# Tokens dealt to partitions in consecutive runs, with z, u and the output in longer rows: attention and a gated layer on one core

## The chip, the cores and the metric

One core of a Trainium2 chip. The metric is the device time of one execution in microseconds (us). Ratios are computed from runs of the same rounds: the mean time of one kernel's fast runs over the mean time of the other's, so a ratio is not quite that of the medians quoted beside it.

## The reference, cut to what matters

```python
# u, v: (8, 3008, 256)  z: (8, 3008, 64)  w_in: (256, 2048)  w_out: (2048, 256), all float32
scores = (1.0 / S) * np.matmul(z, z.transpose(0, 2, 1))
attn = np.maximum(scores, 0.0) ** 2
x = (u * np.matmul(attn, v)).reshape(B * S, D)
h = x @ w_in
return ((h * np.cos(h)) @ w_out).astype(np.float32)      # (24064, 256)
```

Attention sums over all tokens of a batch and nothing depends on a token's place, so any order of tokens will do if z, v, u and the output share it.

## The kernel before, where the change touches it

A batch has 3008 tokens: 23 blocks of 128 and one of 64, which is loaded twice so that it fills 128 partitions. Work goes in 48 slots (8 batches of NC = 6 groups of 512 tokens). A slot has a value phase (`phase_a`, attention times v) and a phase of dense matmuls for earlier slots (`phase_b`). All matmul inputs are float16; loads from GpSimd's queue cast from float32.

```python
    def load_rows(t, src, b, g):                 # v and u: token 128*j + p sits on partition p
        full = 4 if g < NC - 1 else 3
        nc.gpsimd.dma_start(
            t[:, 0:full, :],
            src[b, g * CW:g * CW + full * P, :].rearrange("(j p) d -> p j d", p=P),
        )
        if full == 3:
            for r in range(2):
                nc.gpsimd.dma_start(t[r * H:(r + 1) * H, 3, :], src[b, S - H:S, :])

    def load_v(b, g):
        t = vpool.tile([P, 4, D], FP16, name="v16")       # vpool has 7 buffers, a batch needs 6
        ...
    def emit_turns(due, more=0):                 # transposes of attention pieces A, by SyncE's DMA
        ...
                nc.sync.dma_start_transpose(d.rearrange("p (n j) -> p n j", j=P), a)
    ...
    for s in range(3, NSLOT + 1):
        b, J = s // NC, s % NC
        if s < NSLOT - 2:
            load_u(s + 2)
        ...
            phase_a(s)
        ...
            if J == NC - 2:
                load_v(b + 1, 0)
            if J == NC - 1:                      # the next batch's v, as this batch's buffers come free
                for g in range(1, NC):
                    load_v(b + 1, g)
        ...
        phase_b(s)
```

At the start PE (TensorE) runs seven matmuls on zeros to raise its clock, z of the first batch comes as float32 over the queues of SyncE and ScalarE, is cast, turned on PE, and the first scores go to ScalarE for the relu.

## Time and profile before

| | |
|---|---|
| time, median of 3 (later 6) runs | 1193.71 (1194.28) us |
| PE busy | 1183.3 of 1191.4 us |
| packets under 512 B | 404208 of 479862 |
| queue of SyncE (transposes, output) | 54.4% of the time of 16 DMA engines |
| queue of GpSimd (v, u, z, weights) | 27.3% |

The lines themselves stand in the prediction. Engine shares are averages; what matters is whom PE waits for, and where.

### The profile page before, as it was taken

Reading aid. Unit: us, or ns where it says so; the run is one execution under the profiler, and the core shown is the slowest. Engines: PE = TensorE matmul, PEld = TensorE weight load, DVE = VectorE, ACT = ScalarE, POOL = GpSimd, SP = SyncE. Lnnn points to the kernel's source line nnn. Section 1 sums busy time; section 2 is a strip of 40 time slices with the busy share of each in tenths; the row PEclk is TensorE's granted clock in tenths of the full one; section 3 lists DMA queues with packets and bytes.
Section 4 is the critical chain, followed back from the end, with each engine's and each line's share of the span. In section 5 each row is a group of like instructions: output and inputs, shape, how many; then the busy total and the mean of one; then the engine's idle time right before and its main releaser. Section 6 shows DMA issues by size and latency. Waiting matters only on the chain.

```text
span 1191.4 us, 29044 instructions
## 1 busy us (share of the span) xinstructions
PE 1183.3 (99%) x11887; PEld 727.2 (61%) x11887; DVE 1012.3 (85%) x1302; ACT 794.9 (67%) x927; POOL 690.5 (58%) x717
## 2 busy tenths in 40 slices
PE   9999999999999999999999999999999999999998
PEld 4556665665566656666566665656666566665566
DVE  6899888889988898888988889888888888888776
ACT  7966676667666676667676676666766666666454
POOL 3287746657466573755647556476565665545452
PEclk9999999999999999999999999999999999999999
DMA  9999998569995699946999459973898737964301
GB/s 160 172 170 163 138 147 131 102 121 134 143 130 98 123 140 162 131 84 104 157 147 135 85 104 161 169 119 72 122 164 149 122 71 123 166 125 86 65 20 54
DMA packets 479862, 148.00 MB, mean 124 GB/s; under 512 B 404208, under 2 KB 479472, under 8 KB 479728
## 3 DMA queue, kind: packets, MB, share of 16 engines
q1 hardware_dynamic: 380752, 112.93, 54.4%
q0 software_dynamic: 97440, 32.78, 27.3%
q8 instruction: 93, 1.52, 0.5%
q10 hardware_dynamic: 1536, 0.43, 0.2%
q14 instruction: 41, 0.34, 0.1%
HBM read 66.32 MB, written 24.64 MB: 76 GB/s over the span
## 4 chain that ended last, share of the span: by engine, by line
PE 97%; ACT 1%; DVE 1%; issue 0%; POOL 0%; DVEq 0%; ACTq 0%
PE E L404 27%; PE M L482 23%; PE M L258 20%; PE E L258 19%; PE E L194 5%; PE M L525 1%; ACT r L204 1%; PE M L460 1%; DVE g L415 0%; PE E L664 0%; DVE sm L270 0%; PE E L525 0%; POOL s L433 0%; ACT c L412 0%; DVE o L495 0%
## 5 line engine op out<-in xcount | busy, mean ns | idle before, releaser
L412 ACT ACTIVATE c<-E 128x1024 f16<-128x1024 f32 (+1 forms) x384 | 385.7, 1007 | 216.4 <-PE E L404 214.1
L415 DVE SCALAR_TENSOR_TENSOR g<-E,c 128x1024 f16<-128x1024 f32 (+1 forms) x384 | 458.4, 1195 | 60.6 <-ACT c L412 59.5
L204 ACT ACTIVATE r<-E 128x512 f16<-128x512 f32 (+1 forms) x342 | 327.9, 967 | 112.7 <-PE E L194 106.5
L258 PEld LDWEIGHTS <-v 64*128 64x128 f16 x4512 | 246.3, 94 | 229.3 <-issue 19.4
L404 PE MATMUL E<-x,w_in 128*128 128x512 f16 (+1 forms) x1408 | 354.0, 375 | 0.0
L433 POOL TENSOR_TENSOR s<-g 128x512 f16<-128x512 f16 (+1 forms) x184 | 208.3, 1132 | 188.5 <-DVE g L415 138.7
L258 PE MATMUL M<-A,v 64*128 64x512 f16 (+1 forms) x2256 | 283.0, 372 | 0.2 <-DVE o L495 0.2
L258 PE MATMUL E<-A,v 64*128 64x512 f16 (+1 forms) x2256 | 278.1, 371 | 0.0
L434 POOL TENSOR_TENSOR g<-g 128x512 f16<-128x512 f16 (+1 forms) x184 | 219.5, 1193 | 14.4
L404 PEld LDWEIGHTS <-w_in 128*128 128x128 f16 x1536 | 133.1, 98 | 108.9 <-issue 19.5
L482 PEld LDWEIGHTS <-g 128*128 128x128 f16 x2816 | 172.5, 98 | 40.8
L209 DVE TENSOR_TENSOR A<-r 128x1024 f16<-128x1024 f16 x240 | 174.0, 737 | 15.0 <-ACT r L204 14.3
L286 POOL TENSOR_TENSOR x<-sm,uT 128x512 f16<-128x512 f32 (+1 forms) x43 | 48.6, 1132 | 212.9 <-DVE sm L270 212.5
L482 PEld LDWEIGHTS <-s 128*128 128x128 f16 x2112 | 129.4, 98 | 32.1 <-DVE s L440 0.5
L194 PE MATMUL E<-zT 64*128 64x512 f16 (+4 forms) x684 | 127.6, 355 | 2.0 <-DVE sm L270 0.7
L440 DVE TENSOR_TENSOR s<-s,g 128x1024 f16<-128x1024 f16 (+1 forms) x92 | 100.6, 1094 | 2.1 <-POOL s L433 2.1
L482 PE MATMUL M<-w_mix,s 128*128 128x128 f16 x1408 | 94.0, 219 | 0.3 <-POOL s L433 0.3
L482 PE MATMUL M<-w_mix,g 128*128 128x128 f16 x1408 | 93.6, 219 | 0.0
L482 PE MATMUL M<-w_out,g 128*128 128x128 f16 x1408 | 93.6, 219 | 0.0
L212 DVE TENSOR_TENSOR A<-r 128x512 f16<-128x512 f16 (+1 forms) x102 | 79.6, 781 | 8.9 <-ACT r L204 8.1
L194 PEld LDWEIGHTS <-zT 64*128 64x128 f16 x684 | 38.8, 94 | 38.5 <-issue 4.0
L442 DVE TENSOR_TENSOR s<-g,s 128x1024 f16<-128x1024 f16 (+1 forms) x92 | 60.5, 660 | 0.0
(58 smaller groups left out, 646.9 us busy)
## 6 DMA issues: line engine op xcount, KB each, us to landing
out_dram<-o SPq DMA_DIRECT2D x87, 256.0 KB, 2.2
v<-in_v_dram POOLq DMA_DIRECT2D x40, 256.0 KB, 8.8
u<-in_u_dram POOLq DMA_DIRECT2D x40, 256.0 KB, 4.8
A<-A SPq DMA_TRANSPOSE x252, 5.1
z<-in_z_dram POOLq DMA_DIRECT2D x14, 192.0 KB, 10.6
z<-in_z_dram POOLq DMA_DIRECT2D x14, 176.0 KB, 5.9
v<-in_v_dram POOLq DMA_DIRECT2D x8, 192.0 KB, 11.9
u<-in_u_dram POOLq DMA_DIRECT2D x8, 192.0 KB, 4.1
```

What stands on the lines that cost most here:

```text
L194: nc.tensor.matmul(e[:, t, 0:Wt], zT[rows, k * P:(k + 1) * P], zT[rows, J * CW:J * CW + Wt], start=True, stop=True,)
L204: nc.scalar.activation(r[:, :, 0:W], e[:, :, 0:W], AF.Relu)
L209: nc.vector.tensor_tensor(a4, r4, r4, ALU.mult)
L212: nc.vector.tensor_tensor(a4, r[:, :, 0:W], r[:, :, 0:W], ALU.mult)
L258: nc.tensor.matmul(bank[:, 0:width(J)], vs[b, k // 4][t * H:(t + 1) * H, k % 4, dh * P:(dh + 1) * P], value_rhs(b, J, k, t), start=start, ...
L404: nc.tensor.matmul(e[:, f, 0:W], w_in16[:, k, ft * P:(ft + 1) * P], x[:, k, 0:W], start=(k == 0), stop=(k == 1),)
L412: nc.scalar.activation(c[:, :, 0:W], e[:, :, 0:W], AF.Sin, bias=half_pi, scale=inv_s2)
L415: return lambda: nc.vector.scalar_tensor_tensor(gs[m][:, 2 * i:2 * i + 2, 0:W], e[:, :, 0:W], 1.0, c[:, :, 0:W], ALU.mult, ALU.mult)
L433: nc.gpsimd.tensor_tensor(s1[:, f, 0:n], g[:, f, low], g[:, lower, low], ALU.add)
L434: nc.gpsimd.tensor_tensor(g[:, f, low], g[:, f, up], g[:, f, low], ALU.subtract)
L440: nc.vector.tensor_tensor(s2[:, f, 0:n], s1[:, f, 0:n], g[:, f, up], ALU.subtract)
L482: nc.tensor.matmul(acc[:, k * P:(k + 1) * P], left[:, ft, k * P:(k + 1) * P], right[:, ft, :], start=(ft == 0 and k == 0), stop=(ft == F - ...
```

## The change

The intent is fewer and longer packets. Each half batch (12 or 11 full blocks) is dealt so that partition p owns 12 or 11 consecutive tokens. Four tokens of a partition then lie side by side in HBM, and a transfer can move them as one row where they lie side by side on chip too. v's tile is padded so that its rows don't.

```diff
+    def half_rows(rows, half):
+        lo, hi = halves[half]
+        n = min(hi, NB - 1) - lo
+        return rows[lo * P:(lo + n) * P, :].rearrange("(p j) d -> p j d", p=P)
+
+    def group_rows(rows, g):
+        first = 4 * (g % 3)
+        return half_rows(rows, g // 3)[:, first:first + (4 if g < NC - 1 else 3), :]
 ...
         nc.gpsimd.dma_start(
             t[:, 0:full, :],
-            src[b, g * CW:g * CW + full * P, :].rearrange("(j p) d -> p j d", p=P),
+            group_rows(src[b], g),
         )
 ... (load_z: later z in the same order)
-        t = vpool.tile([P, 4, D], FP16, name="v16")
+        t = vpool.tile([P, 4, D + 16], FP16, name="v16")[:, :, 0:D]
 ... (store_half, last_y: the output)
-            nc.sync.dma_start(
-                out[t0:t0 + n * P, :].rearrange("(k p) d -> p k d", p=P), o[:, 0:n, :]
-            )
+            nc.sync.dma_start(rows[:, 2 * half:2 * half + n, :], o[:, 0:n, :])
 ... (z of the first batch)
-            z[0, g * CW:g * CW + full * P, :].rearrange("(j p) d -> p j d", p=P),
+            group_rows(z[0], g),
```

More of the change, by code (lines that the diff above doesn't have):

```diff
@@ L41 @@
     assert D == 2 * P and dqk == H and S - (NB - 1) * P == H and NB == 4 * NC
-    assert B % 2 == 0 and WL == 3 * P + H and NFT == 16
+    assert NC == 6 and B % 2 == 0 and WL == 3 * P + H and NFT == 16
     inv_s2 = (1.0 / float(S)) * (1.0 / float(S))
@@ L115, in load_z @@
         z16s[b] = z16
-        full = min(hi, NB - 1)
+        n = min(hi, NB - 1) - lo
         for h in range(2):
             nc.gpsimd.dma_start(
-                z16[:, 0:full - lo, h * dqk:(h + 1) * dqk],
-                z[b, lo * P:full * P, :].rearrange("(j p) d -> p j d", p=P),
+                z16[:, 0:n, h * dqk:(h + 1) * dqk], half_rows(z[b], half)
             )
@@ L536, in emit_y, with out_rows @@
                 y_block(m, ft, k)
+    def out_rows(m):
+        b, J = m // NC, m % NC
+        return group_rows(out[b * S:(b + 1) * S, :], J)
     def store_half(m, half, o):
-        b, J = m // NC, m % NC
+        b = m // NC
+        rows = out_rows(m)
         n = min(2, mwidth(m) // P - 2 * half)
-        t0 = b * S + J * CW + half * T
-        if J == NC - 1 and half == 1 and n == 2:
-            nc.sync.dma_start(out[t0:t0 + P, :], o[:, 0, :])
-            nc.sync.dma_start(out[t0 + P:t0 + P + H, :], o[0:H, 1, :])
+        if m % NC == NC - 1 and half == 1 and n == 2:
+            nc.sync.dma_start(rows[:, 2, :], o[:, 0, :])
+            nc.sync.dma_start(out[(b + 1) * S - H:(b + 1) * S, :], o[0:H, 1, :])
             nc.sync.dma_start(out[b * S - H:b * S, :], o[H:P, 1, :])
         else:
-            nc.sync.dma_start(
-                out[t0:t0 + n * P, :].rearrange("(k p) d -> p k d", p=P), o[:, 0:n, :]
-            )
+            nc.sync.dma_start(rows[:, 2 * half:2 * half + n, :], o[:, 0:n, :])
     def store_y(m):
@@ L575, in last_y @@
             )
-            t0 = b * S + J * CW + k * P
             if k < 3:
-                nc.sync.dma_start(out[t0:t0 + P, :], o[:, 0, :])
+                nc.sync.dma_start(out_rows(m)[:, k, :], o[:, 0, :])
             else:
-                nc.sync.dma_start(out[t0:t0 + H, :], o[0:H, 0, :])
+                nc.sync.dma_start(out[(b + 1) * S - H:(b + 1) * S, :], o[0:H, 0, :])
                 nc.scalar.dma_start(out[b * S - H:b * S, :], o[H:P, 0, :])
```

## The prediction

> **What bounds the kernel now.** I read the page's busy table first, then its slices, then the chain that ended last, then the list of waits, and last the timeline of the first 12 us and of the end. The page:
>
> ```profile
> span 1191.4 us, 29044 instructions
> PE 1183.3 (99%) x11887; PEld 727.2 (61%) x11887; DVE 1012.3 (85%) x1302; ACT 794.9 (67%) x927; POOL 690.5 (58%) x717
> ...
> PE   9999999999999999999999999999999999999998
> ...
> DMA  9999998569995699946999459973898737964301
> ...
> DMA packets 479862, 148.00 MB, mean 124 GB/s; under 512 B 404208, under 2 KB 479472, under 8 KB 479728
> q1 hardware_dynamic: 380752, 112.93, 54.4%
> q0 software_dynamic: 97440, 32.78, 27.3%
> ...
> PE 97%; ACT 1%; DVE 1%; issue 0%; POOL 0%; DVEq 0%; ACTq 0%
> ```
>
> PE (TensorE) is busy 1183.3 of 1191.4 us, and 97% of the chain of waits is PE. The DMA row looks alarming (9 in the first six slices and more, some 80% on average), but the PE row beside it is 9 in each of those slices: a full DMA is no bound as long as what it carries comes before PE asks for it.
>
> "Busy" on PE is modelled, so I checked its rate. In the chain in order of time, sixteen half-height value matmuls (64 rows, 512 columns, two of them running side by side) take one fixed time everywhere:
>
> ```profile
> 300.42 1.73 PE E L258 x16
> ```
>
> That is 8 pairs in 1.73 us, 216 ns a pair. One slot of the main loop (there are 48) has 47 such pairs, 32 full matmuls of 512 columns, 112 of 128 columns and 7 score pairs of somewhat under 512 columns. At 216 ns for 512 columns and a quarter of it plus a little (55.6 ns) for 128 this is 10.1 + 6.9 + 6.2 + about 1.4 = 24.6 us. The same group recurs in the chain at 350.16, 374.76 and 399.78 us: 24.60 and 25.02 us apart. So a slot in the middle is matmul issue and nothing else.
>
> What PE itself waits for, in the list of waits of PE (line waited for: us in total, times, longest us):
>
> ```profile
> PE E L664 <- DVE s L627: 1.2, 1, 1.2
> PE E L194 <- DVE sm L270: 0.7, 1, 0.7
> PE E L194 <- DVE g L415: 0.4, 1, 0.4
> PE E L194 <- ACT zT L657: 0.4, 1, 0.4
> ```
>
> No DMA stands there at all. The windows say where PE is idle: 0 to 30 us it is busy 27.32, 30 to 60 29.46, 60 to 209 148.81, 209 to 1100 all 891 us. What the change can shorten is therefore the head, or the last microseconds, in which PE is done and a store is under way.
>
> **What the Trainium skill says.** "TensorE: Matmul & The Clock Gate", section "Wait — 56ns, not 53.3ns?": back to back warm matmuls start every N/2.4 GHz plus about 2.5 ns, 215.7 ns for 512 columns and 55.6 for 128, cold 426.7. The trace agrees: 216 ns a pair above, and the seven warming matmuls at the start take 3.17 us, mostly at some 430 ns. "DMA: Bandwidth & Descriptors", section "Specifications", has 512 B as the smallest transfer for line rate. The trace's packet records, by size, show less of a cliff than a slope: on the queue of GpSimd 128 B packets (z) took 34.1 ns on average, 512 B ones (u, v, w_out) 70.3, 4096 B ones (w_in) 324.8; on SyncE's queue 256 B transpose packets 26.2 and 1024 B output packets 49.3. The same page, "Queues, rings and completion order": each DMA engine goes round its queues packet by packet, so a longer packet makes others wait longer each time; no run here shows this yet.
>
> **The change part by part.** Within each half batch a partition now owns 12 (first half) or 11 (second) consecutive tokens. The same permutation is used for z, u, v and out, attention sums over all tokens and everything later works on single tokens, so the result holds. Built, both programs have the same number of instructions in the same order on every engine (PE 23776 rows, SyncE 377, GpSimd 683); only shapes of transfers differ. No matmul, evacuation or wait is added or removed: the PE time of 1183 us stays.
>
> - u, 48 slots: 4 rows of 256 become one row of 1024 elements. 24576 packets of 512 B (1024 of them for the odd 64 tokens of each batch, loaded twice) become 6144 of 2 KB or 1.5 KB and the same 1024. Time of the 16 engines before: 24576 x 70.3 ns / 16 = 108 us. After (estimate from half of the 324.8 ns of a 4 KB packet): 6144 x 162 / 16 = 62 us, plus 1024 x 70.3 / 16 = 4. About 40 us of 16 engines' time saved, 3.5% of the span. Off PE's path: u's transposes are not in PE's waits.
> - out: 24000 packets of 1 KB become 12000 or so of 2 KB (two tokens at a time, so 2 KB and not more). 24000 x 49.3 / 16 = 74 us becomes perhaps 70. Stores are waited for by nobody except at the end.
> - v: the tile's rows are padded by 16 elements, so that its 1 KB source rows do not merge. Its packets stay 512 B at about 70 ns; gain and loss nil. The padding keeps 2 KB packets of v, which come six slots' worth at once, out of the transposes' way.
> - z of later batches: the source is one long run, but the tile holds two copies of 64 elements side by side, so the pieces written stay 128 B. Nothing.
> - z of batch 0, at the start, on the queues of SyncE and ScalarE: 256 B rows become 1 KB rows. This is the only part on the path. The timeline:
>
> ```profile
> 1.19 3.17 PE L664 MATMUL E<-s 128*128 128x512 f16 x7 [1.19 <-DVE s L627]
> ...
> 3.91 0.80 DVE L645 CAST z<-z 128x512 f16<-128x512 f32 x2 [2.78 <-DMA z<-in_z_dram]
> 4.39 0.60 PEld L649 LDWEIGHTS <-z 128*128 128x128 f16 x8 [0.94 <-DVE z L645]
> ...
> 6.01 3.77 ACT L204 ACTIVATE r<-E 128x1024 f16<-128x1024 f32 x4 [0.49 <-PE E L194]
> ```
>
> The first cast waits for z until 3.91, and PE's first turn of z at 4.39 waits for that cast. For the first block each engine moves 512/16 = 32 packets of 256 B at the measured 21.4 ns on this queue, 0.7 us; as 8 packets of 1 KB at some 50 to 64 ns, 0.4 to 0.5 us. With fewer descriptors to make, z might come 0.2 to 0.5 us sooner. But the seven warming matmuls hold PE: the last starts at 1.19 + 6 x 0.43 = 3.77 and takes 0.43, so PE isn't free before 4.20. At most 0.19 us of the gain reach PE. From 6.01 to about 24 us the chain is the score, its relu on ScalarE (some 1 us each) and the bank's release, which only moves along with its start. Later z blocks, cast on GpSimd, wait for DMA 4.0 us in all, but PE at 9.61 finds them 0.1 us late at most.
>
> The end: the last matmul's evacuation starts at 1187.10, the last stores are issued at 1187.51 and land about 2.2 us later. Their two halves are contiguous rows before and after: 0.
>
> Sum: -0.2 (head, range 0 to -0.5), 0 (middle), 0 (end): 1193.71 - 0.2 = about 1193.5; I put it at 1193.4.
>
> **The rivals.**
> First, that DMA is the hidden bound in the head and the first slots (9s in the DMA row), so that 40 us less engine time lets work go earlier. For: SyncE's transposes take up to 8.6 us to issue, a queue that pushes back, and u's transposes waited 19.4 us for u, 15.6 of it once. Against: that long wait ends at 19.9 us, and nothing on PE waits for it; PE's whole idle time from 12 to 100 us is 1.4 us, ended by DVE and ScalarE. If all of that went, 1192.
>
> Second, that longer packets delay the transposes of A. One 2 KB packet, 162 ns, takes the place of four of 70; in a round between queues a 256 B transpose packet could wait some 90 ns more. For: 47% of the engines' time is these transposes (344960 packets of 26.2 ns), and the value matmuls need them. Against: the total load falls, from about 82% to 78%, and from issue to landing they take 6.0 us in the median while SyncE mostly waits for its producers or for free buffers, hence runs ahead of its consumer; no wait of PE on one is seen. If it bit once per slot in the first eight slots by 0.5 us: 1197.
>
> Third, that a shifted start meets the clock gate differently. "TensorE: Matmul & The Clock Gate", section "What's actually happening", says that the gate's window runs freely. A late release would cost up to half of the first few matmuls, 1 us either way: 1192.5 to 1194.5.
>
> **Range and chances.** The three runs of before span 1193.34 to 1194.58, so 0.6 either side is noise. With the head's gain of 0 to 0.5, the first rival's -1.5 and the second's +3.5 at low weight: 1191.0 to 1195.5 for 8 in 10. A move of 2% is 24 us; all idle time of PE is 8.1 us, so faster is nearly excluded (0.01). Slower by that much needs a new PE stall of half a microsecond in every slot: 0.02. Within 2%: 0.97.
>
> **What would show each step.** Right: PE busy within 1 us of 1183.3, chain 97% PE, slots 24.6 us apart; packets down by about 32000 (17400 from u, 12000 from out, 2200 from the first z); GpSimd's queue from 27.3% to about 24%; the mean DMA share lower; first cast of z before 3.9 us and first turn of z at 4.2 to 4.39. Wrong: a DMA among PE's waits; slots that are longer in the first 200 us than after; transposes of A landing later than the median 6.0 us; or the first turn of z well before 4.2 us, which would mean that the warming matmuls did not hold it.

## The result, and the profile after

1193.12 us (1192.81 to 1193.66, 6 runs) against 1194.28 us (1193.34 to 1195.15, 6 runs): ratio 0.9991, 95% interval 0.9978 to 1.0004. No difference that this can show.

Page of the changed kernel (busy times; busy tenths of PE and of the DMA engines in 40 slices; packets and queues; chain by engine):

```profile
span 1191.2 us, 29044 instructions
PE 1183.7 (99%) x11887; PEld 726.8 (61%) x11887; DVE 1011.5 (85%) x1302; ACT 794.9 (67%) x927; POOL 679.0 (57%) x717
...
DMA  9999999569995799955999469984798837974301
...
DMA packets 449142, 148.00 MB, mean 124 GB/s; under 512 B 401264, under 2 KB 432496, under 8 KB 449008
q1 hardware_dynamic: 368464, 112.93, 56.6%
q0 software_dynamic: 80032, 32.78, 27.7%
...
PE 98%; ACT 1%; DVE 1%; issue 0%; POOL 0%; DVEq 0%; ACTq 0%
```

There are 30720 packets fewer, the DMA engines are not less busy for it (SyncE's queue rose from 54.4 to 56.6%; GpSimd's 27.3 and 27.7% are alike, since second profiles of the same two kernels give 28.2 and 27.3%), and PE is as before: same busy time, and 98% of the chain.

The head, in the timeline of the kernel before (the first scores), then of the changed kernel (first cast of z, first turn, first scores, relu; columns: start, duration, engine, line, instruction, and in brackets the idle time before it and what ended it):

```profile
5.58 0.60 PE L194 MATMUL E<-zT 64*128 64x512 f16 x4 [0.41 <-ACT zT L657]
```

```profile
3.48 1.10 DVE L654 CAST z<-z 128x512 f16<-128x512 f32 x3 [2.35 <-DMA z<-in_z_dram]
...
4.15 1.06 PE L658 MATMUL turned<-id,z 128*128 128x128 f16 x8
...
5.46 1.03 PE L202 MATMUL E<-zT 64*128 64x512 f16 x4 [0.25 <-ACT zT L666]
6.11 3.77 ACT L212 ACTIVATE r<-E 128x1024 f16<-128x1024 f32 x4 [0.71 <-PE E L202]
```

z came 0.43 us sooner (3.91 to 3.48), PE turned it 0.24 us sooner (4.39 to 4.15), and the first relu came 0.10 us later (6.01 to 6.11). In between, the scores took 1.03 us instead of 0.60: PE was at half clock. The clock record of the trace has full clock from 4.66 us in the kernel before and from 6.40 us here.

One thing got worse and cost nothing. Issues of v before, then after (the last number is the median from issue to landing, us):

```profile
v<-in_v_dram POOLq DMA_DIRECT2D x40, 256.0 KB, 8.8
```

```profile
v<-in_v_dram POOLq DMA_DIRECT2D x40, 256.0 KB, 11.5
```

At the end of each batch five loads of v race with PE. I worked out the slack from the trace: for each of the seven batch changes, the start of the first weight load that reads the sixth group of v (in both kernels the tightest of the six at every change), less the landing of that group's last piece. 0 or less is a wait, or a group whose last 64 tokens are read a little later, as at the second change of the changed kernel, where they are read 0.6 us after they land.

| kernel | slack of v's last group at the seven batch changes, us | mean |
|---|---|---|
| before | 6.5, 3.3, 6.4, 2.9, 6.4, 3.7, 0.9 | 4.3 |
| changed | 1.5, -0.2, 1.8, 1.2, 1.0, 1.4, 1.6 | 1.2 |

The second profiles below agree: a mean of 4.5 us for the kernel before, 1.5 us for the changed one. So the change used up some 3 us of a slack that no list of waits shows, and stopped just short of a wait. The experiments are mostly about that.

### The profile page after: what moved, and what is told of

Its sections match the earlier page's. It is cut to its first block, busy times and chain, and to the rows that moved or that the text cites. A ratio compares the mean times of both kernels' runs of the same rounds, so it can differ in the third digit from the quotient of the medians.

```text
span 1191.2 us, 29044 instructions
## 1 busy us (share of the span) xinstructions
PE 1183.7 (99%) x11887; PEld 726.8 (61%) x11887; DVE 1011.5 (85%) x1302; ACT 794.9 (67%) x927; POOL 679.0 (57%) x717
## 3 DMA queue, kind: packets, MB, share of 16 engines
q1 hardware_dynamic: 368464, 112.93, 56.6%
q0 software_dynamic: 80032, 32.78, 27.7%
## 4 chain that ended last, share of the span: by engine, by line
PE 98%; ACT 1%; DVE 1%; issue 0%; POOL 0%; DVEq 0%; ACTq 0%
PE E L412 27%; PE M L490 23%; PE M L266 20%; PE E L266 19%; PE E L202 6%; PE M L533 1%; ACT r L212 1%; PE M L468 1%; DVE g L423 0%; PE E L673 0%; DVE sm L278 0%; PE E L533 0%; POOL s L441 0%; PE M L696 0%; ACT c L420 0%
## 5 line engine op out<-in xcount | busy, mean ns | idle before, releaser
L423 DVE SCALAR_TENSOR_TENSOR g<-E,c 128x1024 f16<-128x1024 f32 (+1 forms) x384 | 458.9, 1197 | 62.0 <-ACT c L420 60.9
## 6 DMA issues: line engine op xcount, KB each, us to landing
v<-in_v_dram POOLq DMA_DIRECT2D x40, 256.0 KB, 11.5
z<-in_z_dram POOLq DMA_DIRECT2D x14, 192.0 KB, 10.9
```

What stands on the lines that cost most here:

```text
L423: return lambda: nc.vector.scalar_tensor_tensor(gs[m][:, 2 * i:2 * i + 2, 0:W], e[:, :, 0:W], 1.0, c[:, :, 0:W], ALU.mult, ALU.mult)
```

## The experiments

Each kernel is a short edit of the changed kernel, unless said otherwise.

**again: the changed kernel unaltered, and aa_before: the kernel before against itself.**

> The changed kernel once more, unaltered, five rounds. My theory (PE's issue time sets the middle, the change can only reach the head): ratio to the kernel before 0.999 to 1.000, interval narrower than the first one. Rival (DMA was a hidden bound somewhere): the 1.1 us of the first comparison stay or grow, 0.998 to 0.999. Second use: one more profile of the head. In the first profile of the changed kernel the scores at 5.46 us ran at half clock (1.03 us for four, against 0.60 before) and the first relu came at 6.11 against 6.01. If that is chance (the clock gate's release), the first relu here lies anywhere in 5.6 to 6.2; if the change causes it, again at about 6.1.

> The kernel before against itself: the noise of such a comparison. Both theories: ratio 1.000 within 0.0005. If it is off by 0.001, the 0.9991 of the change says nothing. Its profile gives a second sample of the head: first cast of z at 3.9 us, first turn at 4.39 us; by the chance reading the first relu may differ from 6.01 by up to 0.4 us, by the other it stays at 6.01.

Measured: again 1193.09 us, ratio 1.0002 (0.9989 to 1.0015; one of its six runs took 1198.53 and is in this ratio; without it the means give 0.9995); aa_before 1193.20 us, ratio 0.9997 (0.9984 to 1.0010). The 0.0009 of the first comparison can't be told from noise. The first relu came at 6.11 us again in the second profile of the changed kernel and at 5.84 us in that of the kernel before. Over all eleven profiles, the clock became full at 4.10 to 6.40 us:

| | clock full at, us |
|---|---|
| first cast after 3.6 us: before, aa_before, pad_only, z_short, all_short | 4.66, 4.18, 5.22, 4.10, 6.24 |
| first cast before 3.6 us: changed, again, v_long, only_v_long, v_pairs, v_long_held | 6.40, 6.01, 4.66, 5.76, 5.69, 6.03 |

Early z tends to go with a late clock, but v_long and all_short are exceptions, so whether the change delays the clock or chance does stays open. In both profiles of the changed kernel the head gained nothing: PE reached the first scores 0.1 us sooner and ran them wholly or partly at half clock. In v_long, where the clock rose early, the first relu came at 5.90 us, 0.1 us sooner than before.

**z_short: the first batch's z by single rows again.**

```diff
-    z32_all = gpool.tile([P, NC, 4, dqk], FP32, name="z32", tag="g")
-    z32 = [z32_all[:, i, :, :] for i in range(NC)]
+    z32_all = gpool.tile([P, NC, 4, dqk + 8], FP32, name="z32", tag="g")
+    z32 = [z32_all[:, i, :, 0:dqk] for i in range(NC)]
```

> The changed kernel with the first batch's z tile padded by 8 elements a row, so that its rows move by themselves (256 B) again; all else as changed. Theory: z lands as before (first cast 3.9 us, not 3.48), and the time is 0 to 0.3 us above the changed kernel's; ratio to the kernel before 0.9995 to 1.000. Rival (the gain is from u and out): time as the changed kernel's, with the head back to 3.9. The packets on ScalarE's queue should be 1408 of 256 B again.

Measured: 1193.25 us, ratio 1.0000 (0.9988 to 1.0012). The first cast is at 3.63 us, not 3.9 (rows of 256 B are not all of the difference), and the first relu at 5.63 us, the earliest of all, because the clock was full at 4.10 us. The long rows of z are worth nothing that can be measured.

**v_long: v without its padding, so in packets of 2 KB like u.**

```diff
-        t = vpool.tile([P, 4, D + 16], FP16, name="v16")[:, :, 0:D]
+        t = vpool.tile([P, 4, D], FP16, name="v16")
```

> The changed kernel without the padding of v's rows: v now moves in 2 KB packets as u does. Theory: PE never waits for A or v, so the time stays within 0.5 us of the changed kernel's, though transposes of A may land later than their median of 6.2 us. Rival (longer packets delay the transposes, and the padding is what saves the change): slower by 2 to 20 us, with a DMA, or a wait on A, among PE's waits at the ends of batches.

Measured: 1217.48 us (1211.99 to 1223.20), ratio 1.0197 (1.0171 to 1.0222). My theory fell: I had expected no change. The waits of v_long (who waited for whom: us, times, longest):

```profile
PEld L266 <- DMA v<-in_v_dram: 24.8, 28, 2.8
...
PE M L266 <- DMA v<-in_v_dram: 11.7, 15, 2.3
```

A DMA stands among PE's waits, and it is v itself, not the transposes of A that the rival named: those landed in 5.0 us in the median, v in 19.2. (The median hides the few transposes beside v. At the second batch change the first took 23.1 us, against 14.5 in the changed kernel; but waits for A add up to 0.7 us.)

```profile
v<-in_v_dram POOLq DMA_DIRECT2D x40, 256.0 KB, 19.2
A<-A SPq DMA_TRANSPOSE x252, 5.0
```

So one padded tile is worth 24 us. (In this profile, a run of 1211.99 us, PE's idle time is 21.7 us in place of the changed kernel's 7.5, and its busy time is 4.8 us longer; at the first late batch the clock also fell to half, from 148.02 to 151.44 us.) Why do four times fewer packets land so much later, in 19.2 us in place of 11.5?

**only_v_long and v_pairs: v's length alone, and half the length.** only_v_long is v_long with u in two transfers of alternate rows and with the padding of z and of the output tile that z_short and all_short show. v_pairs pads after every second row:

```diff
-        t = vpool.tile([P, 4, D + 16], FP16, name="v16")[:, :, 0:D]
+        t = vpool.tile([P, 2, 2 * D + 16], FP16, name="v16")
+        pair = t[:, :, 0:2 * D].rearrange("p a (c d) -> p a c d", c=2)
 ... (the loads and the reads of v by pairs; the last group in one transfer more)
```

> v in 2 KB packets as in v_long, with u, out and the first z by single rows as in the kernel before. Theory (v's own length makes it late): about as slow as v_long, 1207 to 1220, PE waits for v some 20 us. Rival (it is the sum of all long packets, u's and out's too): well below, 1193 to 1200.

> The changed kernel with v's padding after every second row: packets of 1 KB as written, halfway between 512 B (changed) and 2 KB (v_long). Theory (the length of v's packets sets how late v lands, and the changed kernel has 1 to 2 us left at the end of a batch): the last v of a batch lands between that of the changed kernel and that of v_long; PE waits for v a little, 2 to 12 us in all, time 1195 to 1207. Rival (only packets over some length are bad): as the changed kernel, 1193.

Measured: only_v_long 1214.28 us (1204.16 to 1221.24), ratio 1.0167 (1.0113 to 1.0221); PE's weight loads waited 19.8 us for v, which landed in 17.4 us in the median. It is v's own length; u and out have little part in it. v_pairs 1193.23 us, ratio 0.9999 (0.9984 to 1.0014): v landed in 12.4 us, the slack was 2.1, 0.5, -0.3, 2.3, 5.0, 0.4 and 2.2 us (mean 1.8). The list of waits puts 0.8 us of PE's weight loads down to v, but aa_before has the same 0.8 us: it is twice the pause of 0.42 us that weight loads make at a slot's start, and no group of v was late. I had expected a wait of 2 to 12 us; here 1 KB packets behave like 512 B ones, and only 2 KB ones are bad.

**all_short and pad_only: what took the changed kernel's slack.** all_short has the new order of tokens with every row alone. pad_only is the kernel before with v's tile padded and nothing else.

```diff
 # all_short
+        rows = group_rows(src[b], g)
+        for c in range(2 if src is u else 1):
+            n = 2 if src is u else 1
+            nc.gpsimd.dma_start(t[:, c:full:n, :], rows[:, c::n, :])
 ... (z as in z_short)
-opool.tile([P, 2, D], FP32, name="o")
+opool.tile([P, 2, D + 8], FP32, name="o")[:, :, 0:D]
 # pad_only, against the kernel before
-        t = vpool.tile([P, 4, D], FP16, name="v16")
+        t = vpool.tile([P, 4, D + 16], FP16, name="v16")[:, :, 0:D]
```

> The changed order of tokens with every row moving by itself, as in the kernel before (u in two transfers of alternate rows, out and the first z padded, v padded as changed). Theory: time as both kernels, 1193 to 1194; the slack of v at the start of a batch, which fell from 3 to 6 us for the last group before to 1 to 2 us in the changed kernel, comes back to 3 to 6 us if u's and out's long packets took it. Rival: it stays at 1 to 2 us, then the order of the tokens in HBM (steps of 12 KB between partitions) took it.

> The kernel before with v's rows padded apart and nothing else. The kernel with all rows short in the new order of tokens kept only 1 to 3 us of slack for the last v of a batch, against 3 to 6 us before; two things differ from before there, the order of the tokens in HBM and the padding. If the padding took the slack, it is 1 to 3 us here as well; if the order did, it stays 3 to 6 us. Time in both cases as before, ratio 0.999 to 1.001.

Measured: all_short 1194.00 us, ratio 1.0003 (0.9986 to 1.0019); pad_only 1193.17 us, ratio 1.0002 (0.9985 to 1.0019).

| kernel | slack of v's last group, us | mean |
|---|---|---|
| pad_only | 3.2, 5.6, 6.2, 2.9, 6.3, 2.9, 1.6 | 4.1 |
| all_short | 1.3, 3.3, 2.6, 1.3, 0.6, 1.6, 2.2 | 1.8 |

Issues of v in all_short, then in pad_only:

```profile
v<-in_v_dram POOLq DMA_DIRECT2D x40, 256.0 KB, 10.9
```

```profile
v<-in_v_dram POOLq DMA_DIRECT2D x40, 256.0 KB, 8.7
```

The padding costs v nothing; the slack does not come back with short rows of u and out (the changed kernel itself has 1.2 and 1.5 us, z_short 1.7). What is left is the order of the tokens: runs of 4 KB read 12 KB apart (11 KB in the second half) from one partition to the next, in place of 128 rows on end. By elimination, that took most of the 3 us. (u's two transfers in all_short are a second difference, and the order of u, z and out changed with that of v; I separated neither.)

**bench: loads and transposes by themselves.** To measure the disputed cost alone, I wrote a kernel of phases only: six loads of v in rows of 512 B, 1 KB or 2 KB, alone and beside six transposes of 128x2048, all other engines idle, each phase behind a barrier, three times. Its output is wrong, which doesn't matter for the time.

> A measurement by itself, with an output that is wrong on purpose (zeros): six loads with a cast from v, in rows of 512 B, 1 KB or 2 KB as written, first alone, then beside six transposes of 128x2048, and the transposes alone; each phase three times. Theory A (long packets and transposes on the same engines slow each other): alone, six long loads take no longer than six short ones (about 5 to 7 us); beside transposes, the 2 KB packets need over 1.5 times their own time of about 173 ns and the six long loads land at least 1.5 times as late as the six short ones. Theory B (long rows are slow by themselves): the long loads are late alone too. Theory C (it is a matter of where the loads stand in the kernel): no difference between lengths beside transposes.

Last load landed, us after the phase's start:

| rows | alone | beside transposes |
|---|---|---|
| 512 B | 12.1 (one clean phase) | 21.6, 22.1, 20.3 |
| 1 KB | 11.4, 12.5, 11.6 | 16.6, 17.6, 15.6 |
| 2 KB | 10.3, 10.1, 12.3 | 16.2, 13.1, 13.8 |

Theories A, B and C all fell: here the long rows are the fastest, beside transposes too. (The first two phases of 512 B rows collided with my own output stores of 4 KB packets, and needed 36.3 and 42.2 us instead of 12.1.)

**bench2: the same with the other engines at work.** Five loads beside three transposes; the five conditions follow one another.

> A second measurement by itself (output zeros, wrong on purpose). The first one contradicted my reading of v_long: beside transposes with all other engines idle, the 2 KB loads landed sooner (last at 13 to 16 us) than the 512 B ones (20 to 22 us). Here five loads start beside three transposes, with the other engines idle, then with GpSimd, with VectorE, with TensorE and ScalarE, and with all of them at work. Theory D (work on GpSimd or VectorE slows the loads of long rows): idle, the last long load lands at 11 to 16 us as before; with the guilty engine at work at 18 us or later, the short ones 20 us or so throughout. Theory E (none of the engines matters, something of the kernel's own pattern does): long ones at 11 to 16 us in all five conditions.

The conditions were not the planned ones. Nothing made the matmuls and relus wait for their phases, so TensorE and ScalarE worked from the start to 536.5 us, beside the first four conditions, and stood still in most of the last. Two stretches, one of the "idle" condition and one of the last (stretch, its length, then busy us of PE, PEld, DVE, ACT and POOL, then clock, share of DMA, GB/s):

```profile
108.00:125.00 17.00, 10.83 (x38) 3.44 (x36) 1.76 (x39) 17.00 (x20) 2.65 (x5) 1.00 0.93 170
710.00:726.00 16.00, 0.00 (x0) 0.00 (x0) 15.62 (x34) 0.00 (x0) 14.55 (x14) 0.50 1.01 180
```

Read so, the last 2 KB load landed after 13.1, 12.5, 12.8 and 12.8 us with TensorE and ScalarE at work (the conditions meant as "idle" and as theirs), 13.1 and 13.5 with VectorE as well, 11.7 and 12.6 with GpSimd and VectorE alone. (In the condition for GpSimd my barrier let the transposes run ahead of the loads, so it says nothing.) 512 B rows: 19.2 and 17.9 in the "idle" condition. Theory D fell, since GpSimd and VectorE at work delayed no long load; all four engines at once were not measured. Five long loads in GpSimd's timeline, and how they landed:

```profile
109.19 2.65 POOL L78 DMA_DIRECT2D long<-in_v_dram  x5 [14.44 <-DVE long L69]
```

```profile
long<-in_v_dram POOLq DMA_DIRECT2D x5, 256.0 KB, 8.2
dst<-src SPq DMA_TRANSPOSE x3, 8.6
```

**bench3: who starts first, and loads with a pause between.** In v_long the loads go out as buffers come free, 0.8 to 1 us apart. To place the starts I put a small GpSimd instruction behind every load here, which turned out to be the point.

```diff
                 for g, t in enumerate(views(loads)):
                     nc.gpsimd.dma_start(t, rows(loads, phase % 8, g))
+                    pause(128)          # a GpSimd tensor_tensor of 128 columns
```

> A third measurement by itself (output zeros, wrong on purpose). In the changed kernels the transposes start 0.3 us before the first load of v, and while the load of u issued 1.3 us earlier is still under way; in the first two measurements they had the engines to themselves for 0.6 us and more. Here: another load, the transposes, the loads (as in the kernel; the other load with 2 KB packets, then with 512 B packets); transposes and loads alone; and transposes that join two loads under way. Theory F (transposes that start while loads are under way put the engines into the slow mode, worst with 2 KB packets): where they start behind a load, the last 2 KB load lands at 18 us or later, and each transpose and 2 KB packet takes 80 ns and 300 ns or more on average; where they start first, 11 to 16 us. Rival G (who starts first doesn't matter): long ones at 11 to 16 us everywhere, and the cause stays open.

| rows | behind a 2 KB load | behind a 512 B load | transposes start first | transposes join |
|---|---|---|---|---|
| 512 B | 19.9, 20.0 | 20.9, 19.9 | 19.6, 15.8 | 16.7, 16.6 |
| 1 KB | 17.8, 19.6 | 22.6, 20.7 | 19.3, 20.7 | 19.7, 20.2 |
| 2 KB | 24.7, 25.5 | 25.4, 26.4 | 25.1, 23.0 | 20.1, 21.5 |

(us from the phase's start to the last landing; behind another load the phase starts 1.3 us earlier.) The slow mode (long loads that land after 20 us or more, as in v_long) is here, and nearly as late where the transposes start first: so Theory F named the wrong cause, and its rival missed too. Against bench2 the phase "transposes start first" differs by the pause, and by TensorE and ScalarE, which stand still here; but they stood still in the first bench and late in bench2 too, where long loads landed after 11.7 to 16.2 us. GpSimd's timeline shows the loads 0.96 us apart,

```profile
421.13 0.58 POOL L95 DMA_DIRECT2D long<-in_v_dram  x1 [18.01 <-DVE firsts L69]
421.74 0.44 POOL L77 TENSOR_TENSOR work<-work 128x128 f16<-128x128 f16 x1
422.11 0.58 POOL L95 DMA_DIRECT2D long<-in_v_dram  x1
```

and the landing of the same five loads and three transposes is

```profile
long<-in_v_dram POOLq DMA_DIRECT2D x5, 256.0 KB, 20.3
dst<-src SPq DMA_TRANSPOSE x3, 14.2
```

against 8.2 and 8.6 us in bench2. Packets got slow on both sides: the transposes' 256 B packets took 53 and 49 ns on average (21 and 20 in bench2), the 2 KB packets 251 and 214 (210 and 199). Rows of 512 B care little for the pause. (Whether it is the gap that counts, or the GpSimd instruction that fills it, bench3 can't say; in v_long GpSimd waits in the gaps and does nothing.)

**v_long_held: back to back in the kernel.** One line added to v_long:

```diff
             if J == NC - 1:
+                hold(late_sums[-1][0:1, 0:1])      # GpSimd waits for the slot's last sum
                 for g in range(1, NC):
                     load_v(b + 1, g)
```

> v_long (v in 2 KB packets) with one instruction more: at the end of a batch GpSimd waits for the last sum of the slot (some 2 us after the last read of the old v) before it issues the five loads of v, which then go out back to back, 0.53 us apart, instead of one by one as buffers come free, 0.9 us apart. Theory H (2 KB loads issued with gaps beside transposes fall into the slow mode, back to back they don't: 23 to 25 us against 12 to 13 in the measurements by themselves): though issued later, v lands sooner, the last one 12 to 16 us after its issue, PE waits for v some 5 us or less in all, time 1193 to 1200, against 1217 for v_long. If the gaps are not what matters in the kernel, the loads take 20 us again from a later start: 1217 to 1230.

Measured: 1193.55 us (1192.93 to 1194.93), ratio 1.0006 (0.9990 to 1.0023). 24 us are back, by a wait. GpSimd's issue of v at the second batch change, in v_long and then in v_long_held, and v's landing in v_long_held (the median of all batches):

```profile
276.96 0.53 POOL L148 DMA_DIRECT2D v<-in_v_dram  x1 [0.92 <-PE E L202]
277.81 0.53 POOL L148 DMA_DIRECT2D v<-in_v_dram  x1 [0.33 <-PE E L266]
278.74 0.53 POOL L148 DMA_DIRECT2D v<-in_v_dram  x1 [0.40 <-PE E L266]
```

```profile
279.30 0.18 POOL L353 CAST mark<-sm 1x1 f16<-1x1 f32 x1 [7.03 <-DVE sm L278]
279.78 2.64 POOL L148 DMA_DIRECT2D v<-in_v_dram  x5 [0.31 <-PE E L412]
```

```profile
v<-in_v_dram POOLq DMA_DIRECT2D x40, 256.0 KB, 5.4
```

v goes out 5 to 7 us later than in the changed kernel and lands sooner: slack 3.1, 4.2, 3.5, 2.7, 4.4, 3.6 and 3.1 us, mean 3.5, and no wait of PE for v. But two things changed at once. The loads are back to back, and the two large transposes that start at 272.9 and 276.3 us are done (278.2 and 282.0 us) before or soon after v begins. Three smaller ones, from 278.3 us on, still run beside v and end at 290.4, just before v's last landing at 290.7: from v's first packet to its last landing there are 1665 transpose packets in 9.7 us, against 3362 in 24.0 us in v_long. So v did not have the engines to itself, but it met half as many packets, and in the kernel I cannot say which of the two it is. In the measurements by themselves the same transposes ran beside the loads in both, and the pause made the difference. Why gaps put the engines into the slow mode, and whether long loads with gaps are slow without transposes, stays open.

## Why the prediction was right or wrong

- **The bound, and the time: right.** PE's busy time moved by 0.4 us, slots stayed 24.6 us apart (374.61 after 350.01 us in the chain), and 1193.12 us lies 0.3 us from the 1193.4 that I named.
- **"About 40 us of 16 engines' time saved": wrong.** By the packet records u's 2 KB packets took 242.6 ns on average (median 173) and its 1.5 KB ones 195.6, not 162, 90 us in place of the estimated 62. Half of the duration of w_in's 4 KB packets was a fair guess of the median, not of the mean. And a cost is missing from the sum: the new order of tokens. Transpose packets took 25.9 to 26.2 ns in the three profiles of the old order (before, aa_before, pad_only), but 27.9 in the changed kernel and 27.7 in all_short, where no row is long; that is 565 us of engine time before and 600 and 598 after. Packets of u, v and w_out took 225 us before, 243 in all_short, 217 in the changed kernel. So, as far as one profile of all_short shows, the long rows gave back some 26 us and the order cost about 50. (That u has two transfers in all_short is not separated here either.) GpSimd's queue went to 27.7%, not to 24%, and the mean DMA share rose from 82.5 to 85.0%, where it was to fall.
- **"At most 0.19 us of the gain reach PE": nearly right in size, and right that the warming matmuls hold PE** (the last starts at 3.72 us, not 3.77, and the first turn is at 4.15 us, 0.24 sooner, in all six profiles with a first cast at 3.34 to 3.59; z itself came 0.43 us sooner, where the packet times alone gave 0.2 to 0.3), **but the -0.2 us of the sum did not come**: the first relu was 0.1 us later, since the clock rose late. The third rival had named that; I gave it no weight in the sum.
- **"v: gain and loss nil": wrong.** Its landing went from 8.8 to 11.5 us, and its slack from 4.3 to 1.2 us. The step looked at the length of v's packets, which stayed, and left out the order of v's rows, which by elimination is what cost. And I looked at PE's waits only: a transfer with 1 us to spare looks there like one with 40.
- **The padding "keeps 2 KB packets of v ... out of the transposes' way": right that it matters, wrong in whom it protects.** The second rival allowed 1197 us and a late A; without the padding it is 1217 us and a late v. For the kernel as it is, it was right that neither came.

## What to carry to other kernels

A list of waits shows what is late, not what is nearly late: before changing transfers, work out the slack of each load that has a deadline (here v, five loads between the last read of the old batch and the first of the new), and judge the change by it even where the time stays. Fewer and longer packets are no gain by themselves on busy DMA engines; here they moved no time, and on one tensor they cost 24 us. And a load issued as early as its buffer allows can land later than one held back and issued in one run with its neighbours.

## What the Trainium skill lacked or had wrong

- "DMA: Bandwidth & Descriptors", section "Rules for kernel authors", advises to coalesce many small transfers into a large one, and says nothing of a packet that is too long for its neighbours. Here longer packets on v made the kernel 2.0% slower (1217.48 against 1193.42 us). The page has no figure for loads from GpSimd's queue beside DMA transposes: five loads of 2 KB rows landed after 12.5 to 13.1 us back to back and 23.0 to 25.1 us with 0.4 us pauses.
- The same page, "Queues, rings and completion order", has engines going round their queues packet by packet. The measurements agree, if each row of a transfer counts as a packet as it does in the trace (a packet of the page can hold many descriptors), where loads ran beside my 4 KB stores: six loads of 32 packets an engine took about 6.1 us each in place of 1.3, so about 190 ns a packet where the packet itself took 59 and a store's packet 170 to 179. The page does not lead one to expect the slow mode, in which a transpose's packet takes 50 ns instead of 20.
- "TensorE: Matmul & The Clock Gate", section "What's actually happening", gives the point at which the clock rises a spread of 0.5 us either way. Eleven profiles here have it between 4.10 and 6.40 us, after a first matmul at 1.19 us. (The same section also tells of a kernel with 6, 11 or 14 slow matmuls from run to run, which is nearer to this.)
- The same DMA page, "Latency and other measured facts", has a cost of the row pitch in HBM from 512 KiB up. Here, by elimination, loads of 1 KB rows in runs 12 KB apart landed in 10.9 us in place of 8.7 (medians of one profile each).
